# Second scores by one VectorE operation, a feed-forward input of differences, unread products in the head, and a new order

## The chip, the cores and the metric

The kernel runs on one core of a Trainium2 chip. TensorE, VectorE (DVE), ScalarE (ACT), GpSimd (POOL) and SyncE (SP) each work through a queue of their own, in order, and wait for each other by semaphores. The metric is the time of one execution on the device in microseconds, as a median of runs.

## What is computed

```python
B, N, m, C = (4, 12480, 32, 128)
def mab(q, kv):
    s = scale * (q @ kv.transpose(0, 2, 1))
    s = s - s.max(-1, keepdims=True)
    a = np.exp(s)
    a /= a.sum(-1, keepdims=True) + 1e-09
    return a @ kv
h = mab(I, x)                        # 32 inducing points look at 12480 tokens
attn = mab(x, h).astype(np.float32)  # each token looks back at the 32 results
h = attn @ w_in                      # w_in 128 x 2048, w_out 2048 x 128, both float64
g = h - np.tanh(h)
return (g @ w_out).astype(np.float32)
```

## The kernel before

The feed-forward layer is not run on tokens. Its rows are weighted means of 32 rows of h, so it is evaluated once per batch: exactly at the mean of h, and to first order in the differences from it, which gives a 32-row table P4 that the output products read. A test at the end (`bound`, line 640) decides whether that was accurate enough; if not, a general path runs, which it does not here.

Tokens come in steps of 1536 (768 KB), eight for each of four batches, as four quarters of 384 stacked on the 128 partitions, and a remainder for all batches (xR). `first(b)` computes first scores per step on TensorE (line 363), lets VectorE move them to SBUF with the maximum of each row (line 367), joins the maxima of three steps across partitions with small GpSimd copies, VectorE's `nq` between them (`spread` and `back`, lines 376 to 386), takes the exponential (390), transposes it (415) and x (409, 412; 13 of the 32 steps load x in its natural layout as `xn` instead), and accumulates h (422). `feed(b)` joins the groups (460), gathers (472), divides (478 to 480), centres h as hC (485 to 487) and runs the feed-forward layer on 32 rows (490 to 543). `second(b, s)` multiplies hC with the same x buffer (627), which therefore stays until then; `tail` reduces the maximum (573), takes the exponential from PSUM (575), scales P4 (579), makes the output product in four PSUM banks "o" (587), and divides with VectorE, ScalarE and GpSimd (610 to 619) ahead of the store (623).

The float64 weights arrive as words, 512 KB per piece, in eight pieces that use x buffers too; VectorE decodes each in seven operations (278 to 299). There are 16 x buffers, four e2 tiles for exponentials of second scores, and three PSUM banks "ps" for scores, transposes and the feed-forward layer. All transfers are issued by SP, in order, and each waits there until its buffer is free.

Every operation is added to a plan with its engine, a cost and what it reads and writes. A list of numbers, `ORDER` (line 45), sets the order for all engines at once; `Plan.order` (134) follows it with the costs and lags of its model to hand out buffers.

Of the kernel before, what the change touches and what calls it, by code (L numbers as in the profile page):

```python
# [102 lines left out]
class Plan:  # L103
# [30 lines left out]
    def order(self):  # L134

        free = {tag: [(0.0, t) for t in tiles] for tag, tiles in self.places.items()}
        avail, mode, locked = {"SP": 2.6}, None, 0.0
        ops = [self.ops[n] for n in ORDER]
        for op in ops:
            start = max([avail.get(op.eng, 0.0), *(d.end for d in op.deps)])  # L140
# [5 lines left out]
            cost = op.cost  # L146
# [19 lines left out]
def fused_kernel(ctx, tc, xT, xR, xn, indT, w_in, w_out, out, outR):  # L166
# [685 lines left out]
```

## Time and profile before

| | us |
|---|---|
| median of 3 runs | 196.65 (195.49 to 198.43) |
| the profiled execution | 197.96 |
| its span, first to last instruction | 196.1 |
| busy: TensorE / VectorE / ScalarE / GpSimd | 156.4 / 136.9 / 113.5 / 83.8 |
| moved by DMA | 66.41 MB |

"Busy" is the time in which the engine had an instruction. The DMA share is how much of the time the 16 DMA engines were at work; a little over 1 is a full queue. In a timeline, the bracket at the end of a row tells how long the engine was idle before it and what ended that.

### The profile page before, as it was taken

What the parts mean: (1) busy time and instruction counts of PE and PEld (TensorE: products, weight loads), DVE (VectorE), ACT (ScalarE), POOL (GpSimd) and SP (SyncE); (2) the same over time, 40 slices, a digit from 0 to 9 for tenths busy, and PEclk for the clock granted to TensorE, in tenths of its full rate; (3) what the DMA queues carried; (4) which work ended last, traced back from release to release, by engine and by line L of the source; (5) the groups of instructions that cost most, each with busy time, mean ns of one, the idle gap of its engine ahead of it and who ended that gap; (6) DMA issues with size and microseconds to landing.
All of it is one profiled execution on the core that took longest, in us unless ns stands there. A gap on an engine that the chain in (4) does not pass through costs nothing. (4 is left out here: it accounts for less than half of the span.)

```text
span 196.1 us, 6902 instructions
## 1 busy us (share of the span) xinstructions
PE 156.4 (80%) x2776; PEld 101.9 (52%) x2776; DVE 136.9 (70%) x392; ACT 113.5 (58%) x283; POOL 83.8 (43%) x197
## 2 busy tenths in 40 slices
PE   1698598979989999997989849998997979776200
PEld 1536265855657566744756626666664546455200
DVE  4079778979799597874955655678487777985810
ACT  3335427555576678864929670697547579985300
POOL 4005224713110164365463430585735845866830
PEclk9999879999999999999999996999999999996755
DMA  5999999609999999999999999899997646888891
GB/s 166 360 419 420 412 415 389 238 7 342 401 382 413 411 346 372 399 366 414 362 398 368 411 399 351 283 343 362 425 417 290 264 165 258 333 351 360 329 362 43
DMA packets 12682, 66.41 MB, mean 339 GB/s; under 512 B 1537, under 2 KB 1537, under 8 KB 12641
## 3 DMA queue, kind: packets, MB, share of 16 engines
q1 hardware_dynamic: 12640, 65.88, 87.0%
q8 instruction: 24, 0.39, 0.8%
q14 instruction: 18, 0.14, 0.2%
HBM read 40.31 MB, written 25.56 MB: 336 GB/s over the span
## 5 line engine op out<-in xcount | busy, mean ns | idle before, releaser
L619 POOL TENSOR_TENSOR ot<-ot,r 128x384 f32<-128x384 f32 x48 | 39.1, 829 | 35.5 <-DVE r L610 9.3
L412 ACT COPY xn<-PS 128x512 f32<-128x512 f32 x57 | 31.8, 588 | 24.4 <-PE PS L409 24.3
L409 PE MATMUL PS<-ident,x 128*128 128x128 f32 x228 | 35.1, 295 | 3.7 <-DMA x<-in_xT 1.6
L409 PEld LDWEIGHTS PS<-ident,x 128*128 128x128 f32 x228 | 25.7, 148 | 18.4 <-ACT xn L412 4.5
L313 PE MATMUL PS<-x,ind_sb 128*32 128x384 f32 x256 | 28.0, 520 | 4.7 <-DMA x<-in_xT 3.6
L378 POOL COPY mq<-mx 32x4 f32<-32x4 f32 (+2 forms) x48 | 10.0, 209 | 48.8 <-DVE s L367 47.2
L313 PE MATMUL PS<-x,hC 128*32 128x384 f32 x256 | 27.2, 497 | 2.2 <-DVE q L529 1.4
L422 PE MATMUL PS<-xn,et 128*32 128x129 f32 x672 | 24.5, 275 | 2.1 <-DMA xn<-in_xn 1.7
L587 PE MATMUL PS<-pw,e 32*128 32x129 f32 x576 | 24.0, 294 | 2.6 <-DVE ot L613 1.3
L613 DVE TENSOR_TENSOR ot<-PS,r 128x768 f32<-128x768 f32 x24 | 22.8, 950 | 4.2 <-DMA out<-ot 3.8
L587 PEld LDWEIGHTS PS<-pw,e 32*128 32x128 f32 x576 | 19.2, 191 | 10.6 <-DVE ot L613 3.4
L615 ACT COPY ot<-PS 128x768 f32<-128x768 f32 x24 | 19.3, 805 | 8.9 <-PE PS L587 4.6
L367 DVE TENSOR_SCALAR_CACHE_REDUCE s<-PS 128x384 f32<-128x384 f32 x32 | 17.6, 551 | 9.7 <-PE PS L313 8.2
L422 PEld LDWEIGHTS PS<-xn,et 128*32 128x32 f32 x672 | 18.6, 110 | 9.6 <-issue 5.2
L573 DVE TENSOR_REDUCE negm<-PS 128x1 f32<-128x384 f32 (+1 forms) x33 | 17.4, 533 | 4.6 <-PE PS L313 2.8
L415 DVE STREAM_TRANSPOSE et<-s 128x384 f32<-128x384 f32 x32 | 17.8, 560 | 2.6 <-ACT s L390 2.6
L385 POOL COPY nb<-nq 32x1 f32<-32x1 f32 x48 | 14.5, 302 | 11.1 <-DVE nq L380 9.6
L619 POOL TENSOR_TENSOR x<-x,r 128x384 f32<-128x384 f32 (+1 forms) x18 | 14.0, 805 | 4.7 <-DVE r L610 1.5
L575 ACT ACTIVATE e<-PS,negm 128x384 f32<-128x384 f32 x24 | 13.6, 585 | 4.2 <-DVE negm L573 3.9
L390 ACT ACTIVATE s<-s,nb 128x1152 f32<-128x1152 f32 (+1 forms) x12 | 13.8, 1149 | 3.0 <-POOL nb L385 2.9
L313 PEld LDWEIGHTS PS<-x,ind_sb 128*32 128x32 f32 x256 | 7.1, 114 | 11.5 <-issue 6.6
L579 ACT ACTIVATE pw<-P,w 128x129 f32<-128x129 f32 x32 | 12.7, 413 | 0.1
(129 smaller groups left out, 197.6 us busy)
## 6 DMA issues: line engine op xcount, KB each, us to landing
x<-in_xT SPq DMA_DIRECT2D x32, 768.0 KB, 8.0
out<-ot SPq DMA_DIRECT2D x24, 768.0 KB, 6.5
xn<-in_xn SPq DMA_DIRECT2D x13, 792.0 KB, 8.1
out<-x SPq DMA_DIRECT2D x8, 768.0 KB, 4.5
x<-in_w_in SPq DMA_DIRECT2D x4, 512.0 KB, 11.9
x<-in_w_out SPq DMA_DIRECT2D x4, 512.0 KB, 10.0
xR<-in_xR SPq DMA_DIRECT2D x1, 384.0 KB, 3.2
outR<-x SPq DMA_DIRECT2D x1, 384.0 KB, 5.5
```

The source lines that it names most:

```text
L313: nc.tensor.matmul(ps[q * m:(q + 1) * m, :n], lhsT=w(q) if callable(w) else w, rhs=row, start=True, stop=True)
L367: add("DVE", 0.48, lambda ps=ps, k=k, s1=s1, mx=mx: nc.vector.tensor_scalar(out=s1.get()[:, k, :], in0=ps.get()[:, :SEG], scalar1=1.0, sca ...
L385: nc.gpsimd.tensor_copy(nbs.t[q * m:(q + 1) * m, g:g + 1], nq.t)
L409: nc.tensor.transpose(out=ps.get()[:, j * 128:(j + 1) * 128], in_=x.get()[:, (4 * h + j) * 128:(4 * h + j + 1) * 128], identity=ident)
L412: add("ACT", 0.48, lambda ps=ps, xn=xn, h=h: nc.scalar.copy(out=xn.get()[:, 4 * h:4 * h + 4, 0:128], in_=ps.get().rearrange("p (j c) -> p ...
L415: add("DVE", 0.49, lambda s1=s1, et=et, k=k: nc.vector.transpose(out=et.get().rearrange("p k i -> p (k i)"), in_=s1.get()[:, k, :]), reads ...
L422: nc.tensor.matmul(hacc.get()[q * m:(q + 1) * m, g * 130:g * 130 + 129], lhsT=et.get()[:, j, :], rhs=xn.get()[:, j, 0:129], start=(k == 0 ...
L573: add("DVE", 0.08 + T / 960, lambda: nc.vector.tensor_reduce(out=mcol, in_=ps.get()[:, :T], axis=AX.X, op=ALU.max, negate=True), reads=[ps ...
L587: nc.tensor.matmul(o.get()[:BL, q, k * 129:(k + 1) * 129], lhsT=e2.get()[p, k * BL:(k + 1) * BL], rhs=pw.get()[p, 0:129], start=True, stop ...
L613: add("DVE", 0.06 + nv * T / 960, lambda: nc.vector.tensor_tensor(out=res(0, nv), in0=ov(0, nv)[:, :, :, :128], in1=wide(0, nv), op=ALU.mult),
L615: add("ACT", 0.12 + (NQ - nv) * T / 1340, lambda: nc.scalar.copy(out=res(nv, NQ), in_=ov(nv, NQ)[:, :, :, :128]), reads=[o, ot], writes=[c ...
L619: add("POOL", 0.05 + T / 520, lambda q=q: nc.gpsimd.tensor_tensor(out=res(q, q + 1).rearrange("p q k c -> p (q k) c"), in0=res(q, q + 1).r ...
```

## The change

Four edits and a new order.

1. Second scores: one VectorE operation writes the negated scores to the e2 tile and their minimum to `negm`; the exponential then works in place on e2 with scale -1.
2. Feed-forward: the first product reads hA, the differences of h's columns from its last column and the mean as the last one, so that the masks CC and the products with them become four plain transposes. Two PSUM tiles per batch (psT, psR) become parts of psP.
3. In batch 0 ScalarE makes the small copies `spread` and `back`; the first of the seven decoding operations moves from VectorE to ScalarE.
4. Where the plan sees TensorE idle before the first output product, products are issued that nobody reads. Eleven come out of it: eight at the start, three singly.

The planner counts a transfer in its own way now, with a time for issue, one for the start, and a queue. `STAGED` is an empty range, so `weight` takes x buffers as before.

```diff
+HOPS = (0,)
+FILL = (1.0, 0.5)
+STAGED = range(0, 0)
...
-1 2 3 69 0 77 4 73 21 70 74 80 75 72 71 92 76 22 94 23 83 78 95 24 93 25 90 81 26 91 29 27 82 28 37 84 79 101 85 117
+1 2 3 13 80 69 14 73 15 77 16 75 17 0 4 74 81 5 76 70 82 83 18 92 19 71 78 72 93 20 94 45 6 79 105 95 7 90 106 8 117
...
+ISSUE, BEGIN = (0.45, 0.9), 3.3
...
+            if op.eng == "SP":
+                issued = max(start, issued + ISSUE[0])
+                start = max(avail["SP"], issued + ISSUE[1])
+                if lag == LAG["SP"]:
+                    queued = start - issued > ISSUE[1] + 0.5
+                    cost = 1.026 * cost + (0.0 if queued else 0.3)
+                    lag = 1.95 if queued else 0.75
...
-        v.tensor_tensor(out=CC[:, :, 0:m - 1], in0=i4[:, :, 0:m - 1],
-                        in1=i4[:, :, m - 1:m].to_broadcast([128, NQ, m - 1]), op=ALU.subtract)
-        v.tensor_reduce(out=CC[:, :, m - 1], in_=i4, axis=AX.X, op=ALU.add)
-        v.tensor_scalar(out=CC[:, :, m - 1], in0=CC[:, :, m - 1], scalar1=1.0 / m, scalar2=None, op0=ALU.mult)
...
             def magnitude(raw=raw, e=e):
-                nc.vector.tensor_scalar(out=e().bitcast(U32), in0=raw()[:, 1::2], scalar1=0x7FFFFFFF, scalar2=None, op0=ALU.bitwise_and)
+                nc.scalar.activation(out=e(), in_=raw()[:, 1::2].bitcast(F32), func=AF.Abs)
...
+            def copy(dst, src, hop=hop):
+                (nc.scalar.copy if hop else nc.gpsimd.tensor_copy)(out=dst, in_=src)
...
-        def centre():
+        def part():
             v = nc.vector
             v.tensor_reduce(out=hm.t, in_=hU[:, b, :], axis=AX.X, op=ALU.add)
-            v.tensor_scalar(out=hm.t, in0=hm.t, scalar1=-1.0 / m, scalar2=None, op0=ALU.mult)
-            v.tensor_scalar(out=hC[:, b, :], in0=hU[:, b, :], scalar1=hm.t, scalar2=SC, op0=ALU.add, op1=ALU.mult)
+            v.tensor_scalar(out=hA.t[:, 0:m - 1], in0=hU[:, b, 0:m - 1], scalar1=hU[:, b, m - 1:m], scalar2=None, op0=ALU.subtract)
+            v.tensor_scalar(out=hA.t[:, m - 1:m], in0=hm.t, scalar1=1.0 / m, scalar2=None, op0=ALU.mult)
+        add("DVE", 0.2, lambda: nc.vector.tensor_scalar(out=hC[:, b, :], in0=hU[:, b, :], scalar1=hA.t[:, m - 1:m], scalar2=SC,
+                                                       op0=ALU.subtract, op1=ALU.mult),
...
-        add("PE", 0.88, lambda: scores(psU.get(), hU[:, b, :], [win_sb[:, j * 512:(j + 1) * 512] for j in range(NU)]),
+        add("PE", 0.88, lambda: scores(psU.get(), hA.t, [win_sb[:, j * 512:(j + 1) * 512] for j in range(NU)]),
...
             for k in range(4):
-                for q in range(NQ):
-                    n = k * 128 + q * m
-                    nc.tensor.matmul(psM.get()[q * m:(q + 1) * m, k * 128:(k + 1) * 128], lhsT=us.get()[:, n:n + m],
-                                     rhs=CC.rearrange("p q i -> p (q i)"), start=True, stop=True)
+                nc.tensor.transpose(out=psM.get()[:, k * 128:(k + 1) * 128], in_=us.get()[:, k * 128:(k + 1) * 128], identity=ident)
...
-        add("DVE", 0.08 + T / 960, lambda: nc.vector.tensor_reduce(out=mcol, in_=ps.get()[:, :T], axis=AX.X, op=ALU.max, negate=True),
-            reads=[ps], writes=[stat_b[n]], pri=("s2", b, s))
-        add("ACT", 0.17 + T / 1250, lambda: nc.scalar.activation(out=e2.get()[:, :T], in_=ps.get()[:, :T], func=AF.Exp, bias=mcol),
-            reads=[ps, stat_b[n]], writes=[e2], pri=("s2", b, s))
+        add("DVE", 0.08 + T / 960, lambda: nc.vector.tensor_scalar(
+            out=e2.get()[:, :T], in0=ps.get()[:, :T], scalar1=-1.0, scalar2=None, op0=ALU.mult, op1=ALU.min, accum_out=mcol),
+            reads=[ps], writes=[e2, stat_b[n]], pri=("s2", b, s))
+        add("ACT", 0.1 + T / 1150, lambda: nc.scalar.activation(out=e2.get()[:, :T], in_=e2.get()[:, :T], func=AF.Exp, scale=-1.0, bias=mcol),
+            reads=[stat_b[n]], writes=[e2], pri=("s2", b, s))
...
+    idle, begun = FILL[0], False
     for op in plan.order():
+        if op.eng == "PE":
+            begun = begun or op.key[0] == "o"
+            for _ in range(0 if begun else min(8, int((op.start - idle) / FILL[1]))):
+                nc.tensor.matmul(PS[:, 7, :120], lhsT=ident, rhs=ident[:, :120], start=True, stop=True)
+            idle = max(idle, op.start + op.cost)
         op.fn()
```

Of the new order, three places. SP's queue at its start, before (x0, x1 and so on are x buffers; those loaded from in_w are weights, from in_xT tokens):

```order
L318 DMA xR_126<-in_xR 128x768
L231 DMA ind_sb_67<-in_indT 128x32
L357 DMA x0_81<-in_xT 128x1536
L275 DMA x1_82<-in_w_in 128x1024
L357 DMA x2_83<-in_xT 128x1536
L357 DMA x3_84<-in_xT 128x1536
L275 DMA x4_85<-in_w_in 128x1024
L275 DMA x5_86<-in_w_out 128x1024
```

The same place of the change:

```order
L289 DMA x0_80<-in_w_in 128x1024
L371 DMA x1_81<-in_xT 128x1536
L332 DMA xR_125<-in_xR 128x768
L371 DMA x2_82<-in_xT 128x1536
L246 DMA ind_sb_66<-in_indT 128x32
L289 DMA x3_83<-in_w_in 128x1024
L371 DMA x4_84<-in_xT 128x1536
L289 DMA x5_85<-in_w_out 128x1024
```

The first weight moved from fourth to first, the small load of the inducing points (ind_sb) from second to fifth.

SP's queue where the x buffers come round for the second time, before:

```order
L357 DMA x1_82<-in_xT 128x1536
L357 DMA x5_86<-in_xT 128x1536
L357 DMA x4_85<-in_xT 128x1536
L357 DMA x13_94<-in_xT 128x1536
L275 DMA x9_90<-in_w_out 128x1024
L397 DMA xn1_98<-in_xn 128x1584
L275 DMA x10_91<-in_w_out 128x1024
L397 DMA xn3_100<-in_xn 128x1584
L357 DMA x11_92<-in_xT 128x1536
```

The same rows of SP's queue in the change:

```order
L371 DMA x0_80<-in_xT 128x1536
L371 DMA x3_83<-in_xT 128x1536
L371 DMA x10_90<-in_xT 128x1536
L371 DMA x5_85<-in_xT 128x1536
L371 DMA x7_87<-in_xT 128x1536
L289 DMA x11_91<-in_w_out 128x1024
L416 DMA xn1_97<-in_xn 128x1584
L416 DMA xn3_99<-in_xn 128x1584
L371 DMA x4_84<-in_xT 128x1536
```

Five loads into decoded buffers stand ahead of one late weight, where there were four ahead of two; the first load into a buffer that held tokens of batch 0 is the last row of both.

TensorE's queue ahead of the third gather (line 472, of the change 491), before; the products with ind_sb are first scores, with hC second scores, with pw output products, with et the accumulation of h:

```order
L422 MATMUL PS_61<-xn2_99,et1_108 32x129 x12
L409 MATMUL PS_61<-ident_62,x4_85 128x128 x8
L422 MATMUL PS_61<-xn3_100,et2_109 32x129 x12
L313 MATMUL PS_61<-x6_87,ind_sb_67 32x384 x4
L313 MATMUL PS_61<-x5_86,hC_71 32x384 x4
L472 MATMUL PS_61<-fold_63,hsb0_124 32x32 x8
L587 MATMUL PS_61<-pw2_116,e23_113 128x129 x12
```

The same place in the change:

```order
L327 MATMUL PS_61<-x2_82,hC_70 32x384 x4
L609 MATMUL PS_61<-pw2_115,e23_112 128x129 x12
L327 MATMUL PS_61<-x10_90,ind_sb_66 32x384 x4
L491 MATMUL PS_61<-fold_63,hsb0_123 32x32 x8
L466 MATMUL PS_61<-xnR_126,etR3_195 32x129 x2
L327 MATMUL PS_61<-x5_85,ind_sb_66 32x384 x4
L609 MATMUL PS_61<-pw0_113,e20_109 128x129 x12
```

The last first score ahead of the gather reads x10, which is SP's 53rd row in the change; before it was x6, loaded by SP's 56th row. The twelfth output product (of pw2) moved from behind the gather to ahead of it.

## Rows read from the trace of the kernel before

**Rows 1.** Table of stretches: length, busy us (x instructions) per engine, clock, DMA share, GB/s

```profile
10.00:35.00 25.00, 21.12 (x231) 12.04 (x230) 20.53 (x53) 12.16 (x21) 7.15 (x16) 0.93 1.02 410
35.00:46.00 11.00, 9.96 (x172) 7.48 (x160) 9.33 (x26) 5.44 (x12) 4.37 (x10) 1.00 0.39 134
46.00:115.00 69.00, 64.63 (x1199) 41.26 (x1197) 52.01 (x152) 47.22 (x117) 27.32 (x79) 1.00 1.00 388
115.00:125.00 10.00, 7.25 (x104) 4.49 (x96) 5.74 (x21) 3.63 (x11) 1.62 (x2) 0.83 0.89 344
...
150.00:188.00 38.00, 26.43 (x560) 17.78 (x552) 29.38 (x86) 25.56 (x76) 25.83 (x38) 0.90 0.74 295
```

**Rows 2.** SP: timeline (start, us, instruction), then waits (total us, times, longest)

```profile
18.07 25.39 SPq L357 DMA_DIRECT2D x<-in_xT  x6
...
SPq L357 <- DVE win_sb L299: 11.0, 2, 9.8
```

**Rows 3.** Timeline of VectorE in the head

```profile
9.87 0.43 DVE L278 TENSOR_SCALAR x<-x 128x512 uint32<-128x512 uint32 x1 [3.23 <-DMA x<-in_w_in]
...
34.70 0.55 DVE L367 TENSOR_SCALAR_CACHE_REDUCE s<-PS 128x384 f32<-128x384 f32 x1
...
49.27 0.24 DVE L487 TENSOR_SCALAR hC<-hU,hm 128x32 f32<-128x32 f32 x1
```

**Rows 4.** Timeline of TensorE in the head

```profile
21.50 0.41 PE L447 MATMUL PS<-xnR,etR 128*32 128x129 f32 x4 [1.46 <-DVE etR L443]
...
32.37 0.85 PE L313 MATMUL PS<-x,ind_sb 128*32 128x384 f32 x8
...
47.81 0.66 PE L409 MATMUL PS<-ident,x 128*128 128x128 f32 x4
```

**Rows 5.** Timelines of GpSimd and of ScalarE, last group of batch 0

```profile
35.33 1.12 POOL L378 COPY mq<-mx 32x2 f32<-32x2 f32 x4 [3.35 <-DVE s L367]
...
39.86 0.94 ACT L390 ACTIVATE s<-s,nb 128x768 f32<-128x768 f32 x1 [1.88 <-POOL nb L385]
```

**Rows 6.** Timeline of TensorE around 115 us

```profile
111.19 0.95 PE L587 MATMUL PS<-pw,e 32*128 32x129 f32 x24 [0.50 <-DVE nbm L454]
...
118.01 0.85 PE L313 MATMUL PS<-x,ind_sb 128*32 128x384 f32 x8 [2.75 <-DMA x<-in_xT]
...
121.63 1.02 PE L409 MATMUL PS<-ident,x 128*128 128x128 f32 x4
```

**Rows 7.** The x load issued at 43.1 us, and its landing

```profile
L357 SPq DMA_DIRECT2D x<-in_xT x1: 328/328/328, 43.1 to 43.1; - x1
...
DMA to landing us min/median/max: 4.1/4.1/4.1
```

**Rows 8.** Groups by line and shape: xcount | busy us, mean ns | idle before

```profile
L367 DVE TENSOR_SCALAR_CACHE_REDUCE s<-PS 128x384 f32<-128x384 f32 x32 | 17.6, 551 | 9.7 <-PE PS L313 8.2 <-ACT p L540 0.9 <-ACT xn L412 0.3
L573 DVE TENSOR_REDUCE negm<-PS 128x1 f32<-128x384 f32 x32 | 17.0, 540 | 4.6 <-PE PS L313 2.8 <-ACT pw L579 1.8
...
L575 ACT ACTIVATE e<-PS,negm 128x384 f32<-128x384 f32 x24 | 13.6, 585 | 4.2 <-DVE negm L573 3.9 <-PE PS L587 0.3
...
L390 ACT ACTIVATE s<-s,nb 128x1152 f32<-128x1152 f32 x8 | 10.0, 1254 | 1.1 <-POOL nb L385 1.0
...
L612 ACT COPY r<-PS 128x6 f32<-128x6 f32 x32 | 5.3, 171 | 9.3 <-PE PS L587 7.6 <-issue 1.5
...
L502 PE MATMUL PS<-CC,us 128*32 128x128 f32 x128 | 4.3, 275 | 0.1
...
L390 ACT ACTIVATE s<-s,nb 128x768 f32<-128x768 f32 x4 | 3.8, 939 | 1.9 <-POOL nb L385 1.9
...
L367 DVE DVE_READ_ACCUMULATOR s<-PS 128x1 f32 x32 | 2.6, 82 | 0.0
```

**Rows 9.** The x load issued at 50.9 us, and its landing

```profile
L357 SPq DMA_DIRECT2D x<-in_xT x1: 328/328/328, 50.9 to 50.9; - x1
...
DMA to landing us min/median/max: 6.6/6.6/6.6
```

More of the change, by code (lines that the diff above doesn't have):

```diff
@@ L136, in order @@
         free = {tag: [(0.0, t) for t in tiles] for tag, tiles in self.places.items()}
-        avail, mode, locked = {"SP": 2.6}, None, 0.0
+        avail, mode, locked, issued = {"SP": BEGIN}, None, 0.0, 0.0
         ops = [self.ops[n] for n in ORDER]
         for op in ops:
-            start = max([avail.get(op.eng, 0.0), *(d.end for d in op.deps)])
+            start = max([0.0 if op.eng == "SP" else avail.get(op.eng, 0.0), *(d.end for d in op.deps)])
             for x in op.bufs:
@@ L145, in order @@
                     start = max(start, since)
-            cost = op.cost
+            cost, lag = op.cost, op.lag
             if op.mode:
@@ L152, in order @@
                 locked = start + cost
+            if op.eng == "SP":
[5 more added lines that the diff above has]
+                    lag = 1.95 if queued else 0.75
             op.start = start
             avail[op.eng] = start + cost
-            op.end = start + cost + op.lag
+            op.end = start + cost + lag
             for x in op.bufs:
@@ L229, in fused_kernel @@
     ones_b = Buf()
-    add("SP", 0.3, lambda: nc.sync.dma_start(out=ind_sb, in_=indT), writes=[ind_b], pri=("ind",), lag=0.0)
+    add("SP", 0.3, lambda: nc.sync.dma_start(out=ind_sb, in_=indT), writes=[ind_b], pri=("ind",), lag=-0.4)
     add("POOL", 0.6, lambda: make_identity(nc, ident), writes=[ident_b], pri=("ind",))
@@ L257, in masks @@
             v.tensor_scalar(out=F2[:, q, :], in0=fold, scalar1=fv[:, 0:1], scalar2=fv[:, 1:2], op0=ALU.mult, op1=ALU.add)
-    add("DVE", 1.8, masks, reads=[ident_b], writes=[fold_b, cc_b, f2_b], pri=("ind",))
+    add("DVE", 1.4, masks, reads=[ident_b], writes=[fold_b, f2_b], pri=("ind",))
     add("ACT", 0.2, lambda: nc.scalar.activation(out=ind_sb, in_=ind_sb, func=AF.Copy, scale=SC), writes=[ind_b], pri=("ind",))
@@ L264, in weight, with flat, raw, e @@
         for k in range(DFF // n):
-            buf = at("x")
+            buf = at("ot" if first + k in STAGED else "x")
             dst = ws[:, n * k:n * (k + 1)]
-            def raw(buf=buf):
-                return buf.get()[:, :2 * n].bitcast(U32)
-            def e(buf=buf):
-                return buf.get()[:, 2 * n:3 * n]
+            def flat(buf=buf):
+                t = buf.get()
+                return t if len(t.shape) == 2 else t.rearrange("p j d -> p (j d)")
+            def raw(flat=flat):
+                return flat()[:, :2 * n].bitcast(U32)
+            def e(flat=flat):
+                return flat()[:, 2 * n:3 * n]
             def ld(raw=raw, k=k):
@@ L317, in remainder @@
     def remainder():
-        add("SP", 0.9, lambda: nc.sync.dma_start(out=xR_b.t.rearrange("c b n -> c (b n)"), in_=xR), writes=[xR_b], pri=("load r",), lag=1.4)
+        add("SP", 0.9, lambda: nc.sync.dma_start(out=xR_b.t.rearrange("c b n -> c (b n)"), in_=xR), writes=[xR_b], pri=("load r",), lag=-0.3)
         ps = at("ps")
@@ L374, in first, with spread, back @@
             mq, nq = small(f"mq{b}_{g}", [m, NQ, nm]), small(f"nq{b}_{g}", [m, 1])
-            def spread(mx=mx, mq=mq, nm=nm):
+            hop = b in HOPS
+            def copy(dst, src, hop=hop):
+                (nc.scalar.copy if hop else nc.gpsimd.tensor_copy)(out=dst, in_=src)
+            def spread(mx=mx, mq=mq, nm=nm, copy=copy):
                 for q in range(NQ):
-                    nc.gpsimd.tensor_copy(mq.t[:, q, :], mx.t[q * m:(q + 1) * m, :nm])
-            add("POOL", 0.89, spread, reads=[*parts, *([mxR_b] if rem else [])], writes=[mx, mq], pri=p)
+                    copy(mq.t[:, q, :], mx.t[q * m:(q + 1) * m, :nm])
+            add("ACT" if hop else "POOL", 0.4 if hop else 0.89, spread, reads=[*parts, *([mxR_b] if rem else [])], writes=[mx, mq], pri=p, lock=not hop)
             add("DVE", 0.08, lambda mq=mq, nq=nq: nc.vector.tensor_reduce(out=nq.t, in_=mq.t, axis=AX.XY, op=ALU.max, negate=True),
-                reads=[mq], writes=[nq], pri=p, lock=False)
-            def back(nq=nq, g=g):
+                reads=[mq], writes=[nq], pri=p)
+            def back(nq=nq, g=g, copy=copy):
                 for q in range(NQ):
-                    nc.gpsimd.tensor_copy(nbs.t[q * m:(q + 1) * m, g:g + 1], nq.t)
-            add("POOL", 0.89, back, reads=[nq], writes=[nbs], pri=p)
+                    copy(nbs.t[q * m:(q + 1) * m, g:g + 1], nq.t)
+            add("ACT" if hop else "POOL", 0.4 if hop else 0.89, back, reads=[nq], writes=[nbs], pri=p, lock=not hop)
             def ex(s1=s1, n=n, g=g):
@@ L473, in feed @@
         add("PE", 0.46, gather, mode="C", reads=[hsb, fold_b], writes=[ps], pri=("f", b))
-        rs, hm = small(f"rs{b}", [128, m]), small(f"hm{b}", [128, 1])
+        rs, hm, hA = small(f"rs{b}", [128, m]), small(f"hm{b}", [128, 1]), small(f"hA{b}", [C, m])
         def divide():
@@ L481, in feed @@
         add("DVE", 0.72, divide, reads=[ps], writes=[rs, hU_b[b]], pri=("f", b))
-        def centre():
+        def part():
             v = nc.vector
             v.tensor_reduce(out=hm.t, in_=hU[:, b, :], axis=AX.X, op=ALU.add)
-            v.tensor_scalar(out=hm.t, in0=hm.t, scalar1=-1.0 / m, scalar2=None, op0=ALU.mult)
-            v.tensor_scalar(out=hC[:, b, :], in0=hU[:, b, :], scalar1=hm.t, scalar2=SC, op0=ALU.add, op1=ALU.mult)
-        add("DVE", 0.56, centre, reads=[hU_b[b]], writes=[hm, hC_b[b]], pri=("f", b, 1))
+            v.tensor_scalar(out=hA.t[:, 0:m - 1], in0=hU[:, b, 0:m - 1], scalar1=hU[:, b, m - 1:m], scalar2=None, op0=ALU.subtract)
+            v.tensor_scalar(out=hA.t[:, m - 1:m], in0=hm.t, scalar1=1.0 / m, scalar2=None, op0=ALU.mult)
+        add("DVE", 0.45, part, reads=[hU_b[b]], writes=[hm, hA], pri=("f", b))
+        add("DVE", 0.2, lambda: nc.vector.tensor_scalar(out=hC[:, b, :], in0=hU[:, b, :], scalar1=hA.t[:, m - 1:m], scalar2=SC,
+                                                       op0=ALU.subtract, op1=ALU.mult),
+            reads=[hU_b[b], hA], writes=[hC_b[b]], pri=("f", b, 1))
         psU, us = at("ps"), at("us")
-        add("PE", 0.88, lambda: scores(psU.get(), hU[:, b, :], [win_sb[:, j * 512:(j + 1) * 512] for j in range(NU)]),
-            mode="C", reads=[hU_b[b], *win_b], writes=[psU], pri=("f", b))
+        add("PE", 0.88, lambda: scores(psU.get(), hA.t, [win_sb[:, j * 512:(j + 1) * 512] for j in range(NU)]),
+            mode="C", reads=[hA, *win_b], writes=[psU], pri=("f", b))
         add("ACT", 0.5, lambda: nc.scalar.copy(out=us.get(), in_=psU.get()), reads=[psU], writes=[us], pri=("f", b))
@@ L499, in up @@
             for k in range(4):
-                for q in range(NQ):
-                    n = k * 128 + q * m
-                    nc.tensor.matmul(psM.get()[q * m:(q + 1) * m, k * 128:(k + 1) * 128], lhsT=us.get()[:, n:n + m],
-                                     rhs=CC.rearrange("p q i -> p (q i)"), start=True, stop=True)
-        add("PE", 0.9, up, mode="C", reads=[us, cc_b], writes=[psM], pri=("f", b))
-        psT = at("ps")
+                nc.tensor.transpose(out=psM.get()[:, k * 128:(k + 1) * 128], in_=us.get()[:, k * 128:(k + 1) * 128], identity=ident)
+        add("PE", 0.47, up, mode="F", reads=[us, ident_b], writes=[psM], pri=("f", b))
+        psP = at("ps")
         th, gp, q = (small(f"{n}{b}", [128, NF]) for n in ("th", "gp", "q"))
@@ L512, in feed @@
         add("ACT", 0.12, lambda: nc.scalar.activation(out=gp.t, in_=th.t, func=AF.Square), reads=[th], writes=[gp], pri=("f", b))
-        add("ACT", 0.12, lambda: nc.scalar.activation(out=psT.get()[:, :NF], in_=mean(), func=AF.Square), reads=[psM], writes=[psT], pri=("f", b))
+        add("ACT", 0.12, lambda: nc.scalar.activation(out=psP.get()[:, 384:384 + NF], in_=mean(), func=AF.Square), reads=[psM], writes=[psP], pri=("f", b))
         W = at("us")
@@ L530, in series @@
             v.tensor_tensor(out=Wv()[:, :, m - 1], in0=y, in1=t, op=ALU.mult)
-        add("DVE", 0.75, series, reads=[psM, psT, W], writes=[Wg, q], pri=("f", b))
-        psP, P1, psR = at("ps"), at("p1"), at("ps")
+        add("DVE", 0.75, series, reads=[psM, psP, W], writes=[Wg, q], pri=("f", b))
+        P1 = at("p1")
         def down():
@@ L540, in feed @@
         add("ACT", 0.3, lambda: nc.scalar.copy(out=P1.get(), in_=psP.get()[:, :128]), reads=[psP], writes=[P1], pri=("f", b))
-        add("PE", 0.24, lambda: scores(psR.get(), lambda q: F2[:, q, :], [P1.get()] * NQ),
-            reads=[P1, f2_b], writes=[psR], mode="C", pri=("f", b))
-        add("ACT", 0.3, lambda: nc.scalar.copy(out=P4[:, b, 0:128], in_=psR.get()[:, :128]), reads=[psR, ones_b], writes=[P4_b[b]], pri=("f", b))
+        add("PE", 0.24, lambda: scores(psP.get()[:, 128:], lambda q: F2[:, q, :], [P1.get()] * NQ),
+            reads=[P1, f2_b], writes=[psP], mode="C", pri=("f", b))
+        add("ACT", 0.3, lambda: nc.scalar.copy(out=P4[:, b, 0:128], in_=psP.get()[:, 128:256]), reads=[psP, ones_b], writes=[P4_b[b]], pri=("f", b))
         r = slice(b * m, (b + 1) * m)
```

8 lines of the change are left out of this document (3 added, 5 removed), and 66 rows, old and new, of the table ORDER.

## Prediction

> **What bounds the kernel now.** I read the table of stretches first, because no engine is busy to the end. The DMA queue is: its share is 1.02 from 10 to 35 us and 1.00 from 46 to 115 [rows 1]. It idles in three places: 35 to 46 (share 0.39, so 11 x 0.61 = 6.7 us), 115 to 125 (0.89, 1.1 us) and 150 to 188 (0.74, 9.9 us). TensorE is close behind: 64.6 of 69 us between 46 and 115. So two resources are nearly full in the middle, and a gain has to come from the three holes, with TensorE able to follow.
>
> The first hole is the head's doing. From 18 us on SP has six x loads to issue and needs until 43 us for them; the last four go into buffers whose weight VectorE is still decoding, and two of these waits alone come to 11.0 us [rows 2]. VectorE got its first weight at 9.87 us after 3.23 us of waiting for that DMA, and from there works until hC of batch 0 at 49.5 [rows 3]. Inside that chain the eighth score of batch 0 leaves TensorE at 33.2 [rows 4], VectorE takes it up only at 34.70, busy with weights [rows 3], and then GpSimd carries the maximum across partitions and back from 35.33 until ScalarE can start its exponential at 39.86 [rows 5]. The same GpSimd trip kept TensorE idle for 1.46 us at 21.5 [rows 4].
>
> The second hole: at 115.3 TensorE stops for 2.75 us before a first score whose x has not landed, and the next transposes run slow, 1.02 us for four [rows 6] where four take 0.66 elsewhere [rows 4]; the granted clock of that stretch is 0.83 [rows 1].
>
> **The order.** This is the largest part. In SP's queue the first weight now goes first instead of fourth, with the same number of weight bytes and x bytes among the first 26 transfers, but one late weight load instead of two; five reloads of decoded buffers come ahead of it instead of four. TensorE's score before the third gather now reads a buffer loaded by SP's 53rd row; the score that stalled reads the 56th. These change when work starts, not its amount.
>
> Head, to hC of batch 0. (a) VectorE's start: an x load into an idle queue landed 4.1 us after its issue [rows 7], so the weight, issued first, is there near 5 us and decoding starts some 4 us earlier. It is not all gain, since the small ind load is moved behind two x loads and the first score cannot run before it: x loads of 768 KB follow each other by some 1.9 us at 410 GB/s [rows 1], so the first score comes near 12. TensorE therefore starts later but loses fewer waits; I leave the eighth score at 33. (b) VectorE is ahead by then: the 1.5 us between 33.2 and 34.70 goes. (c) The hop of batch 0 moves to ScalarE: GpSimd's took 39.86 - 35.33 = 4.5 us; eight ScalarE copies of [32, few] cost at most 8 x 0.17 us by its smallest copy [rows 8] plus VectorE's small reduction, some 1.5 us, so 3.0 less. ScalarE has room: 5.4 of 11 us in 35 to 46 [rows 1]. (d) One more small VectorE operation stands before hC: +0.2 us. Sum -1.5 - 3.0 + 0.2 = -4.3, hC at 45.2. If TensorE's late start makes the eighth score 2.5 us late, -1.8; if VectorE's head start reaches further, -6.
>
> What that is worth to the DMA: the first reload that needs second scores was issued at 50.9, just after hC, and landed 6.6 us later at 57.5, behind late weights [rows 9]. Issued 4.3 us sooner into a nearly empty queue it lands 4.1 us later, at 50.7: 6.8 us sooner. The hole held 6.7 us in all and some must stay, as nothing can be reloaded between the last decoded buffer and hC. I take **-6.0** (bounds -2 and -8).
>
> Second hole: the load is needed after about as many scores but stands three transfers (some 5.7 us) earlier in the queue, beside the 6 us above. The 2.75 us wait goes; of the DMA's side only its 1.1 us idle counts: **-1.1** (bounds 0 and -2.7).
>
> **Second scores.** 33 reductions of 0.540 us become the form that the first scores already use, 0.551 us plus an accumulator read of 0.082 [rows 8]: +0.09 each, 3.1 us over the run. Against it stand eight magnitudes of 0.43 us [rows 3] that leave VectorE, -3.4. VectorE is level. The PSUM bank comes free after VectorE instead of after the exponential, at least 0.585 us [rows 8] sooner, for TensorE's next score or transpose. That is spread over 33 steps; where TensorE was not waiting for a bank it is worth nothing, so 0 (bound -2). The exponential now reads SBUF. ScalarE's other exponentials do that: 1.254 us for 1152 columns and 0.939 for 768, so 0.315 per 384 and 0.62 for 384, against 0.585 from PSUM [rows 8]: +0.04 x 33 = 1.2 us, hidden, since ScalarE is busy 25.6 of 38 us where it is fullest for long [rows 1].
>
> **Feed-forward and the rest.** Four times, 32 matmul records (4.3 / 4 = 1.08 us [rows 8]) become four transposes (0.66 [rows 4]): -0.4 each. Three of four feeds lie where the DMA is full and give nothing; the last gives **-0.4**.
>
> A page speaks against this edit. The rows first: transposes in the middle of other work take 0.66 us for four [rows 4] in a stretch with granted clock 1.00 [rows 1], the faster of the two levels (2.4 GHz), and 1.02 where the clock of the stretch is down [rows 6]. The Trainium skill (TensorE: Matmul & The Clock Gate, Part 4 on the PE-mode transpose) says that transposes do not bring the array to its full clock and take about 0.275 us each in a kernel. By that four cost 1.1 us, as much as the products that go, and the sum would be -7.1; by the rows it is -7.5.
>
> The differences put some 0.5 us of VectorE work before the first feed product; the second scores of the batch cover it (uncovered: +0.5 x 4). Two PSUM tiles fewer per batch: 0 (bound -1). The three mask operations that go lay before VectorE's idle time ahead of its first weight. Of the eleven unread products eight stand at the very start, where TensorE waits for its first transfer; the others cost below 0.3 us each by [rows 4], in a head bound elsewhere: 0 (bounds -1 for a faster clock, +1). ScalarE gets eight magnitudes, at most 0.6 us each by the price of its exponentials, in a head where it is half idle.
>
> **The end.** One more output step than before lies behind the last batch's gather, and two more stores behind the last load. The DMA's 9.9 idle us in that stretch take in two stores (3.8 us); TensorE's share of them (about 1 us) is taken from the stage ahead. 0, bounds -3 and +3.
>
> Sum: -6.0 - 1.1 - 0.4 = -7.5, span 188.6. TensorE can follow: it sheds 2.75 of waiting, about 1.3 of slow clock (3.6 us at 1.02 for 0.66), 1.7 in four feeds and 4.3 in the head, 10 us. The profiled execution took 197.96 for a span of 196.1, 1.9 more, so 190.5; it lies 1.3 above the median of the runs shown (196.65). In terms of that median: **189.2 us**.
>
> **Rivals.**
> 1. No change: the head isn't shortened. TensorE, blocked by the small load, runs 2.5 us or more late, the decoded buffers come no earlier than now, and the hole stays. For it: the first score waits for the small load behind two x loads, and TensorE's queue is in order. Against: VectorE, not TensorE, ended most of that chain. The head gives -2, the rest -1.5: 193 or more, up to 197.
> 2. Slower: VectorE now needs a free e tile when it reads a second score. There are four, freed when the output products have read them, so VectorE can stand before a score with everything behind it in its queue: first scores, transposes, output products that TensorE waits for. Before, only ScalarE waited there. One full output step is 0.95 us [rows 6]; if VectorE waits that long in every second step, 16 of 33, it costs 15 us, and the time is about 204. It decides from an average of 0.23 us per step (7.5 / 33). Against it: the four tiles rotate, and VectorE has 17 of 69 us to spare between 46 and 115 [rows 1].
> 3. More: TensorE keeps the banks that come free earlier busy, and the end's 9.9 us hole shrinks by half as well: 189.2 - 5 = 184.
> 4. The order was worked out for durations that do not hold: then other stalls of the kind at 115 us appear, 2.75 us each plus the slow clock. Two of them give 189.2 + 2 x 4 = 197.
>
> **How the numbers follow.** The forecast (186 to 192) 0.53; rival 3 (182 to 186) 0.18; rivals 1 and 4 (192.5 to 198) 0.22; rival 2 (over 200) 0.07. The likeliest case's own range is 186 to 192; the one that should hold 8 times in 10 adds most of rival 3 and half of rivals 1 and 4: 183 to 195.5. Faster by over 2% (below 192.7; 2% is about what a measurement of this kernel can tell from no change): 0.53 + 0.18 + 0.02 = 0.73. Within 2%: 0.20. Slower: 0.07.
>
> **What would show it.** Right: the first decode near 5 us; exponential of batch 0's last group within 2 us of the score's reduction; hC of batch 0 at 44 to 47; a DMA hole before 50 us of 1 to 3 us; no TensorE wait over 1 us for an x load after 60 us; the last store's issue near 180. Wrong: VectorE waiting for output products before line 594 (rival 2); hC of batch 0 at 48 or later (rival 1); waits of TensorE for DMA in the middle (rival 4).

## The result and the profile after

The changed kernel takes 190.5 us (median of 4 runs, 188.9 to 191.5) where the kernel before takes 197.1 (195.5 to 198.4): 0.968 of it, 95% interval 0.958 to 0.979. Timed a second time, beside the last experiments, it took 188.9 against 197.5: 0.958 (0.952 to 0.964). Forecast were 189.2, a range of 183 to 195.5, and faster with a chance of 0.73. The profiled execution took 190.7 us for a span of 188.7. The total fits the sum, its terms do not, as the runs below show. Ratios and their intervals leave disturbed runs out and medians do not; where the kernel before scattered (193.6 to 199.7 us beside the joined orders) the two differ by up to 2%, and runs timed beside each other are compared there.

The table of stretches, with the columns of [rows 1]:

```profile
10.00:35.00 25.00, 23.17 (x285) 15.10 (x286) 20.16 (x53) 20.32 (x50) 0.00 (x0) 1.00 0.97 391
35.00:46.00 11.00, 10.93 (x189) 6.71 (x187) 10.28 (x36) 6.75 (x18) 1.56 (x8) 1.00 0.89 317
46.00:115.00 69.00, 65.12 (x1171) 43.52 (x1166) 50.58 (x160) 48.07 (x117) 24.83 (x69) 0.98 0.98 373
115.00:125.00 10.00, 7.61 (x145) 4.28 (x137) 5.85 (x22) 6.29 (x16) 6.25 (x14) 1.00 1.01 398
125.00:150.00 25.00, 23.19 (x497) 15.46 (x495) 20.23 (x69) 15.60 (x47) 14.10 (x32) 1.00 0.92 374
150.00:180.00 30.00, 21.15 (x408) 14.64 (x407) 20.76 (x68) 23.11 (x68) 21.32 (x35) 0.84 0.83 329
```

The hole from 35 to 46 us shrank from 6.7 to 1.2 us (11 x 0.11), the one at 115 is gone. VectorE's timeline shows the head: the first decode, the first score after a wait, the eighth score of batch 0, and hC of batch 0 and of batch 3:

```profile
5.22 0.43 DVE L296 TENSOR_SCALAR x<-x 128x512 f32<-128x512 f32 x1 [2.19 <-ACT x L292]
...
11.54 0.56 DVE L381 TENSOR_SCALAR_CACHE_REDUCE s<-PS 128x384 f32<-128x384 f32 x1 [4.71 <-PE PS L327]
...
33.97 0.56 DVE L381 TENSOR_SCALAR_CACHE_REDUCE s<-PS 128x384 f32<-128x384 f32 x1 [0.28 <-PE PS L327]
...
45.70 0.24 DVE L509 TENSOR_SCALAR hC<-hU,hA 128x32 f32<-128x32 f32 x1
...
145.85 0.20 DVE L509 TENSOR_SCALAR hC<-hU,hA 128x32 f32<-128x32 f32 x1
```

The kernel before had hC of batch 0 ready at 49.5 and that of batch 3, by this row of its VectorE timeline, at 153.2:

```profile
152.92 0.24 DVE L487 TENSOR_SCALAR hC<-hU,hm 128x32 f32<-128x32 f32 x1
```

So 3.6 us are gained by the first of these marks, 7.1 by the last, and 7.4 at the end. In between the lead is not kept. The time at which so many MB had landed (the transfers of a trace added up in the order of their landing; the last two columns are experiments told below):

| MB landed | before | after | new head, old rest | old head, new rest |
|---|---|---|---|---|
| 16 | 53.7 | 47.3 | 47.2 | 50.6 |
| 43 | 123.8 | 121.5 | 122.1 | 123.0 |
| 61 | 180.8 | 171.9 | 182.3 | 172.4 |

At 16 MB the lead is 6.4 us, near the 6.0 that the prediction took for the head. At 43 MB 2.3 of it are left, and the 8.9 at 61 MB come for the most part from somewhere else. The experiments ask where.

### The profile page after: what moved, and what is told of

Read it like the earlier page. It is cut to its first block, busy times and chain, and to the rows that moved or that the text cites. A ratio compares the mean times of both kernels' runs of the same rounds, so it can differ in the third digit from the quotient of the medians.

```text
span 188.7 us, 6747 instructions
## 1 busy us (share of the span) xinstructions
PE 157.4 (83%) x2686; PEld 105.2 (56%) x2686; DVE 133.0 (70%) x418; ACT 122.4 (65%) x315; POOL 71.8 (38%) x173
## 4 chain that ended last, share of the span: by engine, by line
PE 43%; DMA 25%; ACT 12%; DVE 8%; issue 4%; POOL 3%; SPq 1%; ACTq 0%; DVEq 0%
PE PS L327 16%; DMA x<-in_xT 14%; PE PS L609 9%; PE PS L428 8%; PE PS L441 6%; DMA xn<-in_xn 6%; DMA xR<-in_xR 3%; DMA out<-ot 2%; POOL ot L641 2%; ACT xn L431 2%; DVE x L635 2%; ACT x L637 2%; ACT ot L637 2%; PE PS L557 1%; ACT mq L393 1%
## 5 line engine op out<-in xcount | busy, mean ns | idle before, releaser
L327 PE MATMUL PS<-x,ind_sb 128*32 128x384 f32 x256 | 27.2, 506 | 6.7 <-DMA x<-in_xT 5.8
L428 PE MATMUL PS<-ident,x 128*128 128x128 f32 x228 | 31.9, 283 | 0.9 <-ACT xn L431 0.9
L393 POOL COPY mq<-mx 32x4 f32<-32x4 f32 (+2 forms) x36 | 6.6, 183 | 67.7 <-DVE s L381 66.6
L428 PEld LDWEIGHTS PS<-ident,x 128*128 128x128 f32 x228 | 24.6, 142 | 10.4 <-ACT xn L431 4.3
L441 PE MATMUL PS<-xn,et 128*32 128x129 f32 x672 | 25.5, 281 | 1.1 <-DMA xn<-in_xn 0.8
L441 PEld LDWEIGHTS PS<-xn,et 128*32 128x32 f32 x672 | 20.2, 113 | 9.7 <-issue 6.3
L609 PEld LDWEIGHTS PS<-pw,e 32*128 32x128 f32 x576 | 18.6, 186 | 9.5 <-issue 2.5
L609 PE MATMUL PS<-pw,e 32*128 32x129 f32 x576 | 23.1, 287 | 0.5 <-DVE rs L497 0.3
L594 DVE TENSOR_SCALAR_CACHE_REDUCE e<-PS 128x384 f32<-128x384 f32 x24 | 13.0, 543 | 4.7 <-PE PS L327 3.1
L597 ACT ACTIVATE e<-e,negm 128x384 f32<-128x384 f32 x24 | 14.5, 612 | 0.0
L632 DVE RECIPROCAL r<-PS 128x6 f32<-128x6 f32 (+1 forms) x33 | 6.0, 184 | 11.7 <-PE PS L609 11.5
```

Of the source, the lines that this page charges most:

```text
L327: nc.tensor.matmul(ps[q * m:(q + 1) * m, :n], lhsT=w(q) if callable(w) else w, rhs=row, start=True, stop=True)
L428: nc.tensor.transpose(out=ps.get()[:, j * 128:(j + 1) * 128], in_=x.get()[:, (4 * h + j) * 128:(4 * h + j + 1) * 128], identity=ident)
L441: nc.tensor.matmul(hacc.get()[q * m:(q + 1) * m, g * 130:g * 130 + 129], lhsT=et.get()[:, j, :], rhs=xn.get()[:, j, 0:129], start=(k == 0 ...
L597: add("ACT", 0.1 + T / 1150, lambda: nc.scalar.activation(out=e2.get()[:, :T], in_=e2.get()[:, :T], func=AF.Exp, scale=-1.0, bias=mcol), r ...
L609: nc.tensor.matmul(o.get()[:BL, q, k * 129:(k + 1) * 129], lhsT=e2.get()[p, k * BL:(k + 1) * BL], rhs=pw.get()[p, 0:129], start=True, stop ...
```

## The experiments

An order is a list of operations for all engines, so two lists can be cut and joined: the first operations from one, all others in the sequence of the other. An operation that finds no free bank or buffer at its place then stands behind the one that frees it. The diffs are shortened; for a list they say in words what it becomes.

**Order and edits apart.** First all edits in the old order, with the old planner's account of transfers:

```diff
-        ORDER = ...
+        ORDER = old order, part behind divide
```

> All edits of the change, in the order of the kernel before (with its planner's model of transfers; where the longer hold of an e tile or of the one feed-forward bank does not let an operation stand where it stood, it moves behind: 8 operations, by at most 22 places). My theory (the order carries the gain, the hop on ScalarE helps it in the head): hC of batch 0 some 3 us earlier than 49.5, because the hop still shrinks, first reload issued some 3 us earlier, the wait near 115 us stays: 193 to 194 us, so 3 to 4 of the 7.4 us. Rival (the edits bring it themselves, by banks freed earlier and a lighter VectorE): 190 to 191.5 us. Second rival (the order alone): 196 to 197 us.

198.0 us against 197.1: 1.011 of the kernel before (1.004 to 1.018). The edits bring nothing in the old order, as the second rival has it. hC of batch 0 is earlier (47.7), but TensorE waits for the same x load near 115 and then for an xn load (its timeline):

```profile
117.48 0.85 PE L320 MATMUL PS<-x,ind_sb 128*32 128x384 f32 x8 [3.35 <-DMA x<-in_xT]
...
148.19 0.87 PE L434 MATMUL PS<-xn,et 128*32 128x129 f32 x24 [3.36 <-DMA xn<-in_xn]
```

Then the order with as little else as it can do with:

```diff
-        add("DVE", 0.08 + T / 960, lambda: nc.vector.tensor_reduce(out=mcol, ...
+        add("DVE", 0.08 + T / 960, lambda: nc.vector.tensor_scalar(out=e2.get()[:, :T], ... accum_out=mcol), ...
-        ORDER = ...
+        ORDER = new order without part
```

> The kernel before with two parts of the change alone: the new order with its model of transfers, and the second scores by one VectorE operation (without it the order cannot be followed). The hop of batch 0 stays on GpSimd, the magnitudes on VectorE, the feed-forward products and its separate banks stay, no unread products. My theory: hC of batch 0 loses the hop's 2.5 to 3 us against the changed kernel (near 48.5), the reload and the end follow by most of it, the middle runs as in the changed kernel: 192.5 to 194 us. Rival (the edits): 195.5 to 197 us. Second rival (the order alone): 190.5 to 191.5 us.

192.2 us: 0.977 (0.972 to 0.983), 4.9 us less than the kernel before, though hC of batch 0 is not earlier than there (49.5, in a profiled execution of 197.8 us, 5.6 above the median). So the order, with the second scores that it needs, makes most of the gain without a shorter head. The other edits add some 2 to 4 us on top of the new order (0.977 to 0.968 and 0.958), and nothing to the old one.

**The second scores undone.**

```diff
-        add("DVE", 0.08 + T / 960, lambda: nc.vector.tensor_scalar(out=e2.get()[:, :T], ... accum_out=mcol), ...
+        add("DVE", 0.08 + T / 960, lambda: nc.vector.tensor_reduce(out=mcol, ...
```

> The changed kernel with one part undone: second scores by reduction and exponential from PSUM again. With three banks the new order cannot be followed then; each operation goes as early as its bank allows, which moves 435 of 993 operations, by at most 35 places. My prediction priced the operation itself at nothing (bound 2 us): 190 to 192.5 us if the head and the order of the loads carry the gain. Rival (a bank freed one exponential earlier is what lets TensorE follow): 194 us or more, with TensorE's waits for ScalarE's exponential spread over the 33 steps, some 0.1 to 0.2 us in each.

260.6 us, 1.331 (1.323 to 1.338). TensorE's largest waits by cause (us in total, times, longest):

```profile
PE PS L327 <- ACT e L596: 7.6, 7, 1.9
...
PE PS L327 <- ACT s L596: 5.1, 3, 2.7
```

The exponential (line 596 there) holds the bank that the next score needs. The size is not a price of the operation: 137 operations had to move behind their place, and nobody made that order. The two rows are 12.7 of the 70 us that it lies above the changed kernel; the rest was not followed. What it shows is that this order cannot stand without a bank freed by VectorE, not that no other order for the old scores could do as well.

**The hop.**

```diff
-HOPS = (0,)
+HOPS = ()
```

> The changed kernel with the hop of batch 0 back on GpSimd, the order as it is. My theory: the exponential of batch 0's last group comes 2.4 us later (4.5 in place of 2.1), and so hC (48.3 in place of 45.9), the first reload and the rest: 192.5 to 193.5 us. Rival (the first reload waits for the queue of late loads before it, not for hC): hC later all the same, but the time within 0.7 us of the changed kernel's 190.5.

192.0 us, 0.972 (0.964 to 0.979), 1.5 and 3.0 above the two timings of the changed kernel, neither of which stood beside this one; they differ by 1.5 themselves, so the price of the hop is not firm. hC of batch 0 comes 1.1 us later, not 2.4. GpSimd's timeline in this run, then ScalarE's, then VectorE's:

```profile
34.88 1.27 POOL L393 COPY mq<-mx 32x2 f32<-32x2 f32 x4 [4.44 <-DVE s L381]
36.38 1.39 POOL L393 COPY nb<-nq 32x1 f32<-32x1 f32 x4 [0.24 <-DVE nq L399]
```

```profile
37.80 0.94 ACT L409 ACTIVATE s<-s,nb 128x768 f32<-128x768 f32 x1 [1.75 <-POOL nb L393]
```

```profile
46.82 0.24 DVE L509 TENSOR_SCALAR hC<-hU,hA 128x32 f32<-128x32 f32 x1
```

In the kernel before, the same four copies back took 3.14 us:

```profile
36.69 3.14 POOL L385 COPY nb<-nq 32x1 f32<-32x1 f32 x4 [0.24 <-DVE nq L380]
```

**Where in the order.** Three joined orders, all with all edits.

```diff
-        ORDER = new order
+        ORDER = new order up to hC of batch 0, then the old one
```

> All edits; the new order up to hC of batch 0 (the first 205 operations), behind it the order of the kernel before (8 operations moved behind, by at most 22 places, as in the run with all edits in the old order, 1.011 of the kernel before). My prediction (the head brings 6.0 of 7.5 us, and keeps them): 190.5 to 192.5 us. Rival, read from the trace of the changed kernel (its lead over the kernel before is 6 us when 16 MB are moved, 2.3 us at 43 MB and 8.7 us at 61 MB, so that the head's gain is mostly given back and the end makes the rest): hC at 45.9, but 194 to 196.5 us.

197.9 us against 198.0, ratio 1.014 (1.006 to 1.023): no gain, as with the same edits in the old order throughout (1.011). hC stands at 45.7, and the hole of the head is gone, but all of the lead is given back (two rows of the stretches, then TensorE's timeline):

```profile
35.00:46.00 11.00, 10.93 (x187) 6.51 (x185) 10.28 (x35) 6.47 (x16) 1.56 (x8) 1.00 0.92 326
...
115.00:125.00 10.00, 8.48 (x92) 4.44 (x96) 4.22 (x19) 2.65 (x7) 1.67 (x3) 0.66 0.72 255
```

```profile
116.47 1.51 PE L327 MATMUL PS<-x,ind_sb 128*32 128x384 f32 x8 [3.17 <-DMA x<-in_xT]
...
137.81 0.87 PE L441 MATMUL PS<-xn,et 128*32 128x129 f32 x24 [2.42 <-DMA xn<-in_xn]
```

```diff
-        ORDER = new order
+        ORDER = old order up to hC of batch 0, then the new one
```

> All edits; the order of the kernel before up to hC of batch 0 (the first 205 operations), behind it the new order, without another change. My prediction: the 6.0 us of the head are gone but for the hop, 194.5 to 196.5 us. Rival (the order behind the head makes the gain): hC near 47.7, and 191.5 to 193.5 us.

191.8 us, 6.0 below the run with the new head and the old rest, timed beside it; ratio 0.988 (0.979 to 0.998) against 1.014. hC of batch 0 stands at 46.7, so the edits alone keep 2.8 of the 3.6 us at that mark, but the old head's hole is still there (share 0.59 from 35 to 46). hC of batch 3 comes at 146.3, as in the changed kernel:

```profile
35.00:46.00 11.00, 10.94 (x190) 7.10 (x190) 9.96 (x31) 7.06 (x17) 1.83 (x8) 1.00 0.59 218
```

```profile
146.07 0.20 DVE L509 TENSOR_SCALAR hC<-hU,hA 128x32 f32<-128x32 f32 x1
```

The rival is right: the order behind the head makes most of the gain, some 6 us. What the new head adds to it lies between 1 and 4 us: 191.8 stands against 190.5 and 188.9 for the changed kernel, timed at other times, and 0.988 against 0.970 for the run with the ind load moved (below), timed beside it and later found equal to the changed kernel. The spans of single profiled executions (188.4 against 188.7 and 187.9) show no difference.

```diff
-        ORDER = new order
+        ORDER = old order up to hC of batch 2, then the new one
```

> All edits; the order of the kernel before up to hC of batch 2 (623 operations, near 122 us), behind it the new order (2 operations moved behind, by at most 7 places). My prediction gave the end 0 (bounds -3 and +3): 196 to 198 us, as with the old order throughout. Rival (the end makes 5 to 6 us, by fewer waits between hC of batch 2 and the last store): 192 to 194 us.

206.2 us, 1.048 (1.032 to 1.064): slower than either order, so it tells nothing about the end alone. The two lists differ in 45 operations at the cut, which lies behind the 605th operation of the old list, and one x load then lands at 133.6 instead of 125. An order of loads and an order of scores from different plans do not fit.

**One load.** A table of the x loads of batch 3 against the scores that read them (the number of a row in SP's queue gives the load) shows what differs. The kernel before loads step 6 (landed 105.7) for a score at 128.9, and step 4 (landed 117.9) for the score that stalls [rows 6]; all later scores stand behind that stall, the last at 129.9. In the changed kernel the last five loads land almost in the order of need, four of them 1 to 4 us ahead of their scores and one 11, and the last score is taken at 124.5. Lying unused is not by itself the cost: in the changed kernel steps 2 and 1 of batch 3 land 27 and 47 us ahead of their scores. In the kernel before, a load that was needed sooner stood behind the unused one. VectorE's rows for that score, before and after:

```profile
129.92 0.56 DVE L367 TENSOR_SCALAR_CACHE_REDUCE s<-PS 128x384 f32<-128x384 f32 x1 [0.53 <-PE PS L313]
```

```profile
124.52 0.56 DVE L381 TENSOR_SCALAR_CACHE_REDUCE s<-PS 128x384 f32<-128x384 f32 x1 [3.51 <-ACT pw L601]
```

So the two loads were exchanged in the kernel before, which is two numbers of its list:

```diff
-567 299 441 762 ... 312 760 455 608 813 757
+567 299 441 762 ... 312 760 455 608 789 757
...
-475 494 771 768 621 617 511 445 619 618 789 770 ...
+475 494 771 768 621 617 511 445 619 618 813 770 ...
```

> The kernel before with two numbers of its order exchanged and nothing else: in SP's queue the x load of batch 3, step 4 (issued 110.2, landed 117.9, read by the score that stalled TensorE for 2.75 us) and that of step 6 (issued 98.3, landed 105.7, read only at 128.9) change places. Theory formed on the runs so far (TensorE is the engine that sets the third gather and the end, and the one load out of the order of need is what costs it): the wait at 115 goes, the last first score, now at 129.9, comes 3 to 4 us sooner, 192.5 to 194.5 us. My prediction priced this hole at 1.1 us: near 195.5. Rival (the stall comes back at the next late load, or the queue sets the end whatever TensorE does): 196 to 197.5 us.

194.2 us against 197.5: 0.986 (0.979 to 0.992), for one exchange 3.3 us by medians and 2.8 by the ratio (1.6 to 4.1). TensorE's timeline no longer stops there:

```profile
115.07 0.87 PE L422 MATMUL PS<-xn,et 128*32 128x129 f32 x24
115.75 0.83 PE L313 MATMUL PS<-x,ind_sb 128*32 128x384 f32 x8
116.40 0.83 PE L313 MATMUL PS<-x,hC 128*32 128x384 f32 x8
```

The same exchange in the order with the new head:

> The run with all edits, the new order up to hC of batch 0 and the old one behind it (1.014 of the kernel before, hC at 45.7), with the same two x loads of batch 3 exchanged. Theory: the head's lead was lost in the stall at 113; without the stall most of it reaches the end: 190.5 to 193 us. Rival (the lead is lost elsewhere in the old order, in the full DMA queue before 113 or in the waits for xn behind it): 194 to 197 us.

194.4 us, 0.987 (0.982 to 0.992), some 3.5 below the run without it. But it is no faster than the exchange in the kernel before, whose hC of batch 0 is some 2 us later (48.9 against 47.0). Head and edits together bring nothing in the old order, stall or no stall: the second half of the theory falls.

**TensorE's late start.**

```diff
-    add("SP", 0.3, lambda: nc.sync.dma_start(out=ind_sb, in_=indT), ...
+    add("ACT", 0.1, lambda: nc.scalar.dma_start(out=ind_sb, in_=indT), ...
```

> The changed kernel with its small ind load issued first, from ScalarE's own DMA queue, instead of behind two x loads on SP. My theory (TensorE's late start was a cost of the head that VectorE's early start only hid): first score near 6 to 7 us instead of 9.96, eighth score of batch 0 and hC 1 to 2 us sooner, time 0.5 to 2 us below the changed kernel's 190.5. Rival (VectorE's weights and TensorE's transposes fill the head, the late first score costs nothing): hC within 0.5 us of 45.9, time the same.

188.6 us and a span of 184.3, which looked like 2 us of gain. It was run once more, with the changed kernel beside it.

> The changed kernel itself, beside which the other runs of this call are read: 0.968 of the kernel before, as first timed.

> The changed kernel with the small ind load issued first from ScalarE's own queue, beside the changed kernel on the same chip. If its 188.6 us were its own merit: 1.5 to 3 us below the changed kernel. If they were the chip's: within 1 us of it.

189.1 us, 0.959 (0.954 to 0.965), against 188.9 for the changed kernel: the same. The first score moved by 0.4 us only, because the products with the remainder xR stand ahead of it (TensorE's timeline), and hC stayed at 46:

```profile
7.69 1.97 PE L355 MATMUL PS<-ident,xR 128*128 128x128 f32 x8 [2.55 <-DMA xR<-in_xR]
9.58 1.51 PE L327 MATMUL PS<-x,ind_sb 128*32 128x384 f32 x8
```

No version here beats the changed kernel.

## Why the prediction came out, step by step

**The head's chain: right, its parts partly.** hC was to come 4.3 us sooner and came 3.6 sooner (45.9 for 49.5). The first decode is at 5.2, as forecast. The hole left before 50 us is 1.2, within the forecast of 1 to 3. VectorE takes the eighth score 0.7 us sooner (33.97 for 34.70), not 1.5: TensorE ends it at 33.8, where it was to stay near 33. The hop takes 2.1 us, not 1.5: the ScalarE copies cost 0.2 us each, above the bound of 0.17. From the exponential to hC it is 0.4 us less, not 0.2 more. A magnitude takes 0.70 us on ScalarE, where at most 0.6 was forecast.

```profile
34.57 0.80 ACT L393 COPY mq<-mx 32x2 f32<-32x2 f32 x4 [0.79 <-DVE s L381]
...
35.87 0.79 ACT L393 COPY nb<-nq 32x1 f32<-32x1 f32 x4
36.69 0.94 ACT L409 ACTIVATE s<-s,nb 128x768 f32<-128x768 f32 x1
```

And of the 4.5 us that GpSimd took before, less belonged to GpSimd than I charged: with the same copies on GpSimd the new order needs 2.9 (34.88 to 37.80), so the engine is worth 1.1 us at hC and not 3.0.

**"What that is worth to the DMA ... I take -6.0": wrong.** This is the step that failed. The transfers did come 6.4 us sooner at 16 MB. I counted that as time off the end, because the queue is full from 46 to 115 us. But a queue whose loads wait for buffers is not a fixed amount of work to be started sooner. With the new head and the old order the lead was 1.7 us at 43 MB and the end did not come sooner (197.9 against 198.0); with the old head, the new rest alone made 6.0 us. The term measures 0 in the old order and 1 to 4 in the new one. The marks in the traces tell where the lead goes: of 3.6 us at hC of batch 0 only 1.5 are left at hC of batch 1.

| end of hC, batch | before | after | new head, old rest | old head, new rest | before, two loads exchanged |
|---|---|---|---|---|---|
| 0 | 49.5 | 45.9 | 45.7 | 46.7 | 48.9 |
| 1 | 82.7 | 81.2 | 81.0 | 82.0 | 82.2 |
| 2 | 122.9 | 118.7 | 123.4 | 120.5 | 120.1 |
| 3 | 153.2 | 146.1 | 155.1 | 146.3 | 152.3 |

The last column is of a profiled execution of 197.0 us, 2.8 above that run's median.

**The second hole, -1.1: too small.** "Of the DMA's side only its 1.1 us idle counts" was the error: I measured a TensorE stall by the idle time of the queue. Taken away alone, by one exchange, it gave 2.8 to 3.3 us, about the 2.75 of the wait.

**The end, 0: right.** From hC of batch 3 to the end it is 42.9 us before and 42.6 after, and all other traces but that of the second scores undone (71) lie between 41 and 45. So the time is that of this mark plus some 42 us. In the changed kernel and with the old head before the new rest the mark comes 7 us sooner, of which the exchange explains some 3. The rest is made between hC of batch 2 and hC of batch 3: 25.7 and 27.4 us in the two columns that end in the new order, 30.2 to 32.2 in the three that end in the old one. It may lie in the xn loads: TensorE waits for one until 137.8 and 148.2 in the two runs above that end in the old order, and until 148.1, for 0.95 us, in the kernel before, and for none in that stretch of the changed kernel (one of 0.8 at 129), which has issued 10 of the 13 by hC of batch 2 where the kernel before had 8. That is read from the traces, not shown by a run.

**The second scores, 0 (bound -2): right as an operation, wrong as a part of the whole.** The durations hold; the exponential from SBUF takes 0.612 for an estimate of 0.62 (groups by line and shape, count, busy, mean ns, idle before):

```profile
L597 ACT ACTIVATE e<-e,negm 128x384 f32<-128x384 f32 x24 | 14.5, 612 | 0.0
L594 DVE TENSOR_SCALAR_CACHE_REDUCE e<-PS 128x384 f32<-128x384 f32 x24 | 13.0, 543 | 4.7 <-PE PS L327 3.1 <-PE PS L609 1.5
```

But I asked what a bank freed earlier is worth to the old sequence of work. Here its worth is that the new sequence becomes possible.

**The feed, -0.4, and the page.** Four transposes between other work took 0.66 us, where the granted clock was 1.00 (46 to 60 us); the second row is of all sixteen, with the mean duration of one:

```profile
54.10 0.66 PE L523 MATMUL PS<-ident,us 128*128 128x128 f32 x4
...
L523 PE MATMUL PS<-ident,us 128*128 128x128 f32 x16 | 2.6, 286 | 0.3 <-ACT us L515 0.3
```

The Trainium skill (TensorE: Matmul & The Clock Gate, Part 4) gives some 0.275 us for each in a kernel and says that transposes do not bring up the clock. One lasts 0.286 us here, near the page's figure, but the next starts before it ends, so four cost 0.66 and not the 1.1 that the prediction drew from the page. Whether transposes alone would bring up the clock no run here shows: other products stand around them. What the edit is worth to the time was not measured, nor were the unread products and the moved magnitudes undone one by one.

**Rivals.** Rival 2 left one mark, the 1.5 us behind "PE PS L609" in the row above: VectorE waited once for an e tile. Rival 1's "the first score waits for the small load" is at most 0.7 of the 4.71 us that VectorE waits there: with the load moved, 4.0 remain. What the rest costs stays open. Rival 4 was partly there: TensorE waits 2.02 us for an x load at 91 and 1.61 at 123, against "no TensorE wait over 1 us for an x load after 60 us". Behind the first of them the granted clock fell: it was 0.50 from 92 to 95 us, and 24 products that took 0.87 us ahead of the wait took 1.59 behind it.

```profile
88.27 0.87 PE L450 MATMUL PS<-xn,et 128*32 128x129 f32 x24
91.16 0.95 PE L327 MATMUL PS<-x,ind_sb 128*32 128x384 f32 x8 [2.02 <-DMA x<-in_xT]
91.81 1.59 PE L441 MATMUL PS<-xn,et 128*32 128x129 f32 x24
...
123.52 0.85 PE L327 MATMUL PS<-x,ind_sb 128*32 128x384 f32 x8 [1.61 <-DMA x<-in_xT]
```

So -7.5 was met by a head that is worth 4 at most in place of 6, and by an order behind it that is worth some 6 in place of 1.1. Two errors in opposite directions made the sum: that the total came out is luck. The forecast of the marks in the head was good; that of what they are worth was not.

## What to carry to other kernels

Work out for the engine that is nearly always busy which of its waits comes last, and follow that wait to its cause; a lead gained early is worth only what the later waits let through. Look at each load's landing against the use of it: where one lies unused (23 us here) while another, issued behind it, is waited for, an exchange of two entries of the list gains the wait. Ask of an operation that frees a buffer sooner which orders it allows, and judge an order only as a whole: two lists cut and joined gave 206 us.

The Trainium skill (Perfetto Trace Analysis, Identifying Performance Opportunities) says to find the gaps on the engine chosen and what each waits for. The traces here agree: the 2.75 us gap of TensorE was worth some 3 us, the 5.5 us less of idle queue in the head at most 4.

## What the runs showed of the hardware

Four GpSimd copies of [32, 1] took 1.39 us in one order and 3.14 in another, with different VectorE work beside them; four on ScalarE took 0.79. And the length of a wait did not tell what TensorE's clock did behind it. After 2.02 us of waiting, in the changed kernel, the granted clock fell to 0.50, the lower of the two levels (1.2 and 2.4 GHz), from 92 to 95 us. After 3.17 us, in the run with the new head and the old rest, it was 0.50 as well, and eight products took 1.51 us. After 3.35 us, in the run with all edits in the old order, it was 1.00, and the same eight products took 0.85.
